# Maxima over the partitions by a TensorE product with the identity in place of a GpSimd instruction

## The chip, the core and the metric

The kernel runs on one core of a Trainium2 chip. The core has five engines that run their own queues of instructions in order and wait for each other through semaphores: TensorE (PE in the profile; its weight loads are shown apart as PEld), VectorE (DVE), ScalarE (ACT), GpSimd (POOL) and SyncE (SP, which here issues the transfers). The metric is the device time of one execution in microseconds (us).

## What is computed

Four batches of attention with eight heads, 576 tokens and head size 64, in which a score counts only if it is at most tau below its row's maximum; then a gated MLP behind an RMS norm over the 2304 tokens; then a mixture of eight experts whose weights come from a softmax over all the logits and eight Sinkhorn steps. The reference, cut to what matters:

```python
thresh = np.max(scores, axis=-1, keepdims=True) - tau
scores = np.where(scores >= thresh, scores, -1e9)
attn = softmax(scores);  x = attn @ v
xn = x / rms(x) * rms_g
x = (silu(xn @ w_gate) * (xn @ w_val)) @ w_out
P = np.exp(logits - logits.max())            # logits = x @ moe2_w_gate
for _ in range(8):                           # Sinkhorn
    P /= P.sum(1, keepdims=True) + 1e-9
    P /= P.sum(0, keepdims=True) + 1e-9
    P *= N / E
for e in range(8):
    out += P[:, e:e+1] * (np.maximum(x @ w1[e], 0) @ w2[e])
```

## The kernel before, in words

Every float32 operand of a large product is scaled by a power of two and split into two float16 parts, and three passes carry the product. The power of two comes from the largest magnitude of the operand. Along the free axis VectorE finds that maximum, one number for each of the 128 partitions (`kmm`, `vmm`, `om1`, `w1m`, `w2m`, `gm`). The maximum over the 128 partitions, with the result in all of them, is GpSimd's `partition_all_reduce` (`all_max`, L137 to L140). It is called 42 times through `all_max`: for k and v of each batch (`kmx`, `vmx`, 4 each), for w_out (`womx`), for the router's weights (`gmx`), and for w1 and w2 of each of 16 half experts (`w1mx`, `w2mx`). A 43rd call on L704 (`lgtop`) takes the maximum of the logits. From the maximum `pow2_scale` (L70 to L76) makes the scale by five small VectorE instructions; for squared norms GpSimd first takes a square root as a power (L144).

The work comes in three stages. Up to about 200 us of the span, the first batch and the MLP's weights are prepared (`prep_in`, `prep_out`). Up to about 780 us, the attention of a block of tokens is interleaved with the MLP of the block before it (`att_tile`, `mlp_block`): a score tile S on PE, its row maximum and threshold on DVE, the exponential on ACT, the float16 remainder `hl` on POOL (L271, L272), a transposing transfer to `eT`, and the product `pv` on PE; for the MLP, 12 tiles `gv` (24 matmuls each, L488) with a tanh on ACT and two DVE instructions, the remainder `tT` on POOL (L503), and two tiles `x2` (36 matmuls each, L516). From about 870 us on the mixture of experts runs: in each of 16 halves `hidden` makes tiles h (6 matmuls each, L751), and `combine` makes 18 tiles y (12 matmuls each, L797), which ACT (L808) or DVE (L812) adds up. The next half's weights are prepared meanwhile: DVE takes the row maximum (L616, L641), POOL forms sums of blocks (L621 to L624), ACT and DVE split (L604, L605).

PSUM has 8 banks. The pool `psm` gives three to the tag "mm", on which the tiles gv, x2, logits, the Sinkhorn sums cs and y take turns; the attention takes the other five (later the h tiles do). The order of instructions on each engine is made when the program is built, by a scheduler with a timeline of its own, so a change in one place moves instructions on all engines.

Of the kernel before, what the change touches and what calls it, by code (L numbers as in the profile page):

```python
# [7 lines left out]
F32 = mybir.dt.float32  # L8
# [4 lines left out]
ALU = mybir.AluOpType  # L13
# [6 lines left out]
def kernel(  # L20
# [14 lines left out]
):  # L35
    """Attention with a threshold below each row's maximum, a gated MLP behind an RMS norm, and a
    mixture of experts with Sinkhorn weights.

    Each float32 operand of a large product is scaled by a power of two, taken from its largest
    magnitude, and split into two float16 parts, hi + lo, which hold its 22 bits and more; three  # L40
    passes (hi*hi, hi*lo, lo*hi) then carry the product with float32's accuracy. The scales are
    exact, and the bounds that they give keep every float16 value finite.
    """
    nc = tc.nc
# [12 lines left out]
    NW = NCH + 1  # L57
    ABSMAX = bass_isa.ReduceOp.absmax
    MAXOP = bass_isa.ReduceOp.max

# [5 lines left out]
    def pow2_scale(mx, n, bits, name, least=2.0**-100):  # L66
        """2^(bits-1) / 2^floor(log2 mx), so that scaled values stay under 2^bits; and its inverse."""
        s = small([P, n], name + "_s")
        inv = small([P, n], name + "_i")
        V.tensor_scalar(  # L70
            inv.bitcast(I32), mx.bitcast(I32), 0x7F800000, None, ALU.bitwise_and
        )
        V.tensor_scalar(inv, inv, least, None, ALU.max)
        V.reciprocal(s, inv)
        V.tensor_scalar(s, s, 2.0 ** (bits - 1), None, ALU.mult)
        V.tensor_scalar(inv, inv, 2.0 ** (1 - bits), None, ALU.mult)  # L76
        return s, inv
# [4 lines left out]
    V.memset(half, 0.5)  # L82
    ones = small([P, P], "ones")
    V.memset(ones, 1.0)
    tau_sb = small([P, 1], "tau_sb")
    G.dma_start(out=tau_sb, in_=tau.to_broadcast([P, 1]))
# [21 lines left out]

    psm = ctx.enter_context(tc.tile_pool(name="psm", bufs=3, space=PSUM))

# [6 lines left out]

# [1 line left out]
    def load_batch(b, which="kqv"):  # L119
# [16 lines left out]

    def all_max(col, n, name):  # L137
        m = small([P, n], name, bufs=2)
        G.partition_all_reduce(m, col, P, ABSMAX)
        return m  # L140

    def norm_scale(sq, n, bits, name):
        """The scale and its inverse from squared norms."""
        G.tensor_tensor(sq, sq, half.to_broadcast([P, n]), ALU.pow)  # L144
        return pow2_scale(sq, n, bits, name, 2.0**-60)

    def row_norms(r, name):
        """Of each row of r, the largest of the squared norms of its parts."""
        r = r.rearrange("p h c d -> p (h c d)")
# [13 lines left out]
    def prep_kq(b, raws):  # L163
        kr, qr = raws
        st = {}
        s_k, i_k = norm_scale(all_max(row_norms(kr, "km"), 1, "kmx"), 1, 10, f"k{b}")
        qm = small([P, NW], "qm", bufs=2)
# [5 lines left out]
        s_q, i_q = norm_scale(qm, NW, 9, f"q{b}")  # L173
        # of a row's maximum M: -c2 M, the bias of its exponentials, and M - c1, its threshold
        wt = small([P, NW, 2], f"wt_{b}")
# [28 lines left out]
    def prep_v(b, st, vr):  # L204
        s_v, i_v = norm_scale(all_max(row_norms(vr, "vm"), 1, "vmx"), 1, 14, f"v{b}")
        vs = pa.tile([P, 2, H, NW, D], F16, tag="vs", name=f"vs{b}")
        A.activation(vs[:, 0], vr, AF.Copy, scale=s_v[:, 0:1])
        V.scalar_tensor_tensor(
            vs[:, 1].rearrange("p h c d -> p (h c d)"),
            vr.rearrange("p h c d -> p (h c d)"),  # L210
            s_v[:, 0:1],
            vs[:, 0].rearrange("p h c d -> p (h c d)"),
            ALU.mult,
            ALU.subtract,
        )
        st["vs"] = vs
        st["i_v"] = i_v
# [22 lines left out]
    def att_tile(b, c, st, qT, qX, heads, pv, sums, slot):  # L240
        """One 128-row tile of scores: 128 tokens of one head, or the last 64 of two heads."""
        kT, vs = st["kT"], st["vs"]
# [24 lines left out]
        )  # L267
        # columns: hi of keys 0..575 | lo of keys 512..575 | lo of keys 0..511
        hl = pa.tile([P, 2 * S], F16, tag="hl", name=f"hl{b}_{c}_{heads[0]}", bufs=3)
# [26 lines left out]
    def finish_x(i, x, ivx):  # L296
        """RMS norm of the 128 tokens of tile i, split and transposed."""
        ssq = pa.tile([P, 1], F32, tag="ssq", name=f"ssq{i}", bufs=2)
# [15 lines left out]

    # tiles of 128 tokens in the order in which they are made: 128 of a batch (token p * 4 + c), or
    # the last 64 of two batches
    tiles = []
# [47 lines left out]

# [1 line left out]
    wg = pw.tile([P, 2, KD, DFF], F16, tag="wg", name="wg")  # L367
# [6 lines left out]
    def words(src, name):  # L374
        """128 x DM float64 numbers, as pairs of words: the lower, the upper."""
        r = pw.tile([P, 4, 2, 2 * P], F16, tag="tT", name=name, bufs=4)
# [4 lines left out]
    def to_f32(dst, word, name):  # L381
        """Their float32, from their bits.

        2^-112 times the upper word, read as float32, has the exponent rebiased for float32 and
        three places too low; the lower word gives the last three bits of the mantissa.
        """
        lw = pw.tile([P, 2, 2, HD], F16, tag="xs", name=name, bufs=2)
# [11 lines left out]
    def prep_in(src, w, gi, name):  # L399
        """DM columns of w_gate or w_val, times rms_g, scaled for columns of norm under 2^9."""  # L400
        bits = src.bitcast(I32)
# [38 lines left out]
    def prep_out():  # L440
        """w_out, its rows scaled against their columns of w_gate and w_val."""
        bits = moe_w_out.bitcast(I32)
# [15 lines left out]
        V.tensor_reduce(om1, om, AX.X, ALU.max)  # L458
        s, inv = pow2_scale(all_max(om1, 1, "womx"), 1, 8, "wout")
        V.tensor_scalar(ixs, inv, 2.0**10, None, ALU.mult)  # L460
# [16 lines left out]
    def passes(n):  # L477
        """(part of the stationary operand, part of the moving one, chunk) of a split product."""
        return [(l, r, c) for c in range(n) for l, r in ((0, 0), (0, 1), (1, 0))]

    def mlp_block(j, pool=None):
# [30 lines left out]
        for a in range(2):  # L512
# [22 lines left out]
            xs.append(x)  # L535
        # the operands of the products below, from [B11; B21], the first tile, and [B12; B22]
        xl, xr = xs
# [27 lines left out]

# [1 line left out]
    for i, (b, c) in enumerate(tiles):  # L567
# [23 lines left out]

# [1 line left out]
    # Its first layer by Winograd's form of Strassen's product: w1[e]' = A and x' = B are cut in  # L593
    # 2 x 2, and 7 products of their blocks' sums give the 4 blocks of A B. Half an expert's F at
    # a time. Columns of B: a pair of tiles; the sums of B are those that mlp_block kept.
    pb_cm = tc.tile_pool(name="pb", bufs=1, side="left", reuse_waits="tile")
# [5 lines left out]
    def split(dst, src, s):  # L602
        """dst[:, ..., 0, :], dst[:, ..., 1, :] = the float16 parts of src * s."""
        A.activation(dst[0], src, AF.Copy, scale=s)  # L604
        V.scalar_tensor_tensor(dst[1], src, s, dst[0], ALU.mult, ALU.subtract)  # L605

    def prep_w1(h, pool):
# [8 lines left out]
        V.tensor_reduce(m, r, AX.XY, ALU.max, apply_absolute_value=True)  # L616
        s, inv = pow2_scale(all_max(m, 1, "w1mx"), 1, 3, f"w1_{h % 3}")
        a11, a12 = r[:, 0:2, 0:HF], r[:, 2:4, 0:HF]
# [14 lines left out]
    def prep_w2(h):  # L633
# [7 lines left out]
        V.tensor_reduce(m, r, AX.XY, ALU.max, apply_absolute_value=True)  # L641
        s, inv = pow2_scale(all_max(m, 1, "w2mx"), 1, 8, f"w2_{h % 3}")
        split((w[:, 0], w[:, 1]), r, s[:, 0:1])
# [26 lines left out]
    def sinkhorn():  # L670
        """Softmax over all the logits, then rows and columns brought to equal sums in turn."""
        gr = small([P, KD, E], "gr")
        nc.scalar.dma_start(out=gr, in_=moe2_w_gate.rearrange("(k p) e -> p k e", p=P))
        gm = small([P, 1], "gm")
        V.tensor_reduce(gm, gr, AX.XY, ALU.max, apply_absolute_value=True)
        s, inv = pow2_scale(all_max(gm, 1, "gmx"), 1, 8, "gate2")
        wg2 = small([P, KD, 2, E], "wg2", F16)
        A.activation(wg2[:, :, 0], gr, AF.Copy, scale=s[:, 0:1])
        V.scalar_tensor_tensor(wg2[:, :, 1], gr, s[:, 0:1], wg2[:, :, 0], ALU.mult, ALU.subtract)
        ps = psm.tile([P, NTL, 2, E], F32, tag="mm", name="logits")  # L680
        # (operand, chunk of D) whose sum is the tile's x
        parts = (
# [19 lines left out]
        V.tensor_reduce(mx, lg, AX.XY, ALU.max)  # L702
        top = small([P, 1], "lgtop")
        G.partition_all_reduce(top, mx, P, MAXOP)  # L704
        V.tensor_scalar(top, top, -1.0, None, ALU.mult)
# [37 lines left out]
    def hidden(h, g):  # L743
        """The split relu(w1[e]' x') of KH chunks of F: those of the first tiles, of the second."""
        w, xb = weights[h][0], xop[g]
# [126 lines left out]
```

## Time and profile before

| | us |
|---|---|
| median of 3 runs | 2316.86 |
| lowest and highest | 2316.15, 2324.15 |
| span of the profiled execution, first to last instruction | 2318.3 |
| PE busy | 2041.2 (88%) |
| DVE busy | 1532.4 (66%) |
| ACT busy | 817.5 (35%) |
| POOL busy | 583.1 (25%) |

The page gives the profiled execution by its span alone; it lies 1.4 us above the median of the runs, so differences in the span can be taken as differences in time. A busy share is an average over stages: POOL's 25% is gathered in the first third and in bursts later. "issue" as the releaser of a wait means that the engine sat idle and no semaphore that the profile shows explains it.

### The profile page before, as it was taken

To read this page: it belongs to the slowest core of one execution; us is meant where nothing else is said; L and a number is where in the kernel's file an instruction comes from. 1 tells how busy PE (TensorE), PEld (TensorE's weight loads), DVE (VectorE), ACT (ScalarE), POOL (GpSimd) and SP (SyncE) were. 2 spreads that over 40 slices of the span, in tenths; PEclk is the share of its full clock that TensorE was granted. 3 is DMA by queue.
4 is the path that set the end of the run, shared out by engine and by line. 5 is a ranking of instruction groups with operands and counts; after the bars stand their busy time and mean duration, and the time that the engine had idled before them with its cause. 6 is when DMAs were issued, how large, how long until landed. Compare 5 with 4: busy or idle time off the path is not lost.

```text
span 2318.3 us, 35265 instructions
## 1 busy us (share of the span) xinstructions
PE 2041.2 (88%) x13828; PEld 1195.3 (52%) x13828; DVE 1532.4 (66%) x3102; ACT 817.5 (35%) x1450; POOL 583.1 (25%) x677
## 2 busy tenths in 40 slices
PE   1234887888899797799999999999999999999999
PEld 0023675576677564354555555555555555555554
DVE  6797676677777326586676676676676676676555
ACT  4556665575565223222122122122122122122111
POOL 4675465456565322101010010010010010010000
PEclk9998999999999899799999999999999999999999
DMA  7684775785575604100010010010010010010001
GB/s 213 164 197 89 130 157 99 136 151 110 101 132 108 129 17 119 55 17 21 19 37 19 19 37 19 19 37 19 19 37 19 19 37 19 19 37 1 1 27 56
DMA packets 321879, 154.10 MB, mean 66 GB/s; under 512 B 278960, under 2 KB 292400, under 8 KB 321712
## 3 DMA queue, kind: packets, MB, share of 16 engines
q1 hardware_dynamic: 321120, 151.82, 28.9%
q8 instruction: 108, 1.77, 0.3%
q14 instruction: 59, 0.48, 0.1%
q10 hardware_dynamic: 528, 0.02, 0.0%
q0 software_dynamic: 64, 0.00, 0.0%
HBM read 68.18 MB, written 12.98 MB: 35 GB/s over the span
## 4 chain that ended last, share of the span: by engine, by line
PE 63%; issue 3%; DVE 2%; POOL 1%; DMA 1%; ACT 0%; SPq 0%; POOLq 0%; ACTq 0%; DVEq 0%
PE y L797 31%; PE h L751 26%; PE gv L488 3%; PE x L516 2%; DMA w1r<-in_moe_w_dram 1%; DMA eT<-hl 0%; POOL w1s L621 0%; DVE nt L259 0%; PE S L248 0%; DVE mx L257 0%; SPq L653 0%; DVE w L605 0%; PE pv L286 0%; DVE e L265 0%; POOL w1s L623 0%
## 5 line engine op out<-in xcount | busy, mean ns | idle before, releaser
L751 PE MATMUL h<-x2T,w 128*128 128x384 f16 x4032 | 687.9, 326 | 16.4 <-ACT u L765 15.2
L751 PEld LDWEIGHTS <-w 128*128 128x128 f16 x4032 | 394.6, 98 | 298.5 <-issue 18.0
L812 DVE SCALAR_TENSOR_TENSOR acc<-y,coef,acc 128x512 f32<-128x512 f32 x270 | 193.6, 747 | 252.0 <-PE y L797 249.9
L797 PE MATMUL y<-w,hA 128*128 128x512 f16 x864 | 221.8, 382 | 2.1 <-ACT w L604 1.6
L797 PE MATMUL y<-w,hC 128*128 128x512 f16 x864 | 211.2, 381 | 9.7 <-ACT acc L808 9.7
L797 PE MATMUL y<-w,hD 128*128 128x512 f16 x864 | 217.3, 381 | 0.0
L739 ACT ACTIVATE hA<-u 128x384 f16<-128x384 f32 x96 | 50.2, 523 | 456.9 <-DVE u L767 449.4
L797 PE MATMUL y<-w,hB 128*128 128x512 f16 x864 | 210.3, 379 | 0.0
L621 POOL TENSOR_TENSOR w1s<-w1r 128x512 f32<-128x512 f32 x16 | 23.7, 1482 | 737.8 <-DMA w1r<-in_moe_w_dram 722.2
L271 POOL TENSOR_TENSOR hl<-e,hl 128x512 f16<-128x512 f32 x144 | 174.0, 1209 | 121.7 <-ACT hl L270 60.3
L488 PE MATMUL gv<-xnT,wg 128*128 128x256 f16 x1296 | 171.4, 277 | 13.7 <-ACT x2f L534 13.7
L516 PE MATMUL x<-wo,tT 128*128 128x512 f16 x648 | 155.3, 397 | 18.7 <-POOL tT L503 18.7
L488 PE MATMUL gv<-xnT,wv 128*128 128x256 f16 x1296 | 169.6, 274 | 0.0
L248 PE MATMUL S<-kT,qT 128*128 128x288 f16 (+1 forms) x320 | 67.9, 315 | 103.2 <-DVE e L265 73.5
L488 PEld LDWEIGHTS <-wg 128*128 128x128 f16 x1296 | 127.0, 99 | 33.0 <-issue 14.6
L264 ACT ACTIVATE e<-S,nt,c 128x576 f32<-128x576 f32 x144 | 117.3, 824 | 71.5 <-DVE nt L259 60.5
L797 PEld LDWEIGHTS <-hC 128*128 128x128 f16 x864 | 84.7, 98 | 106.9 <-issue 11.1
L797 PEld LDWEIGHTS <-hB 128*128 128x128 f16 x864 | 84.7, 98 | 102.5 <-issue 0.8
L797 PEld LDWEIGHTS <-hD 128*128 128x128 f16 x864 | 84.9, 98 | 98.5 <-issue 2.2
L488 PEld LDWEIGHTS <-wv 128*128 128x128 f16 x1296 | 125.5, 98 | 16.1 <-issue 0.7
L797 PEld LDWEIGHTS <-hA 128*128 128x128 f16 x864 | 85.0, 99 | 94.3 <-issue 4.8
L265 DVE SCALAR_TENSOR_TENSOR e<-S,nt,e 128x576 f32<-128x576 f32 x144 | 115.9, 811 | 26.8 <-ACT e L264 25.9
(237 smaller groups left out, 2884.7 us busy)
## 6 DMA issues: line engine op xcount, KB each, us to landing
w1r<-in_moe_w_dram SPq DMA_DIRECT2D x16, 1024.0 KB, 5.1
w2r<-in_moe_w_dram SPq DMA_DIRECT2D x16, 1024.0 KB, 5.4
wgatew<-in_moe_w_gate_dram SPq DMA_DIRECT2D x12, 512.0 KB, 4.9
wvalw<-in_moe_w_val_dram SPq DMA_DIRECT2D x12, 512.0 KB, 4.2
wo<-in_moe_w_out_dram SPq DMA_DIRECT2D x12, 512.0 KB, 4.4
x2d<-xs SPq DMA_DIRECT2D x24, 256.0 KB, 2.5
qX<-qT SPq DMA_DIRECT2D x40, 128.0 KB, 2.5
raw_k<-in_k_dram SPq DMA_DIRECT2D x4, 1024.0 KB, 7.6
```

The lines of the kernel that those rows point to most:

```text
L248: T.matmul(sp[i * rows : (i + 1) * rows, j, 0:HS], lhsT=qq[:, h, 0:rows], rhs=kT[2 * h // H][:, h % (H // 2), j * HS : (j + 1) * HS], star ...
L264: A.activation(ev, sv, AF.Exp, bias=nt[:, 0:1], scale=st["c2"][:, c : c + 1])
L265: V.scalar_tensor_tensor(ev, sv, nt[:, 1:2], ev, ALU.is_ge, ALU.mult, accum_out=sums[:, slot : slot + 1])
L271: G.tensor_tensor(hl[:, S + REM :], e[:, 0 : NCH * P], hl[:, 0 : NCH * P], ALU.subtract)
L488: T.matmul(gv[:, a, :], lhsT=w[:, l, kk, f * P : (f + 1) * P], rhs=xt[:, r * KD + kk, :], start=n == 0, stop=n == 3 * KD - 1,)
L516: T.matmul(ps, lhsT=tT[f][:, l, o : o + P], rhs=wo[:, f, r, :], start=n == 0, stop=n == 3 * KF - 1,)
L621: G.tensor_tensor(sm[:, 0], a21, a22, ALU.add)
L739: A.activation(t[:, 0, :], src, AF.Relu)
L751: T.matmul(ps, lhsT=w[:, a, l, kk, f * P : (f + 1) * P], rhs=xb[:, b * 4 + r * 2 + kk, :], start=n == 0, stop=n == 5,)
L797: T.matmul(ps, lhsT=hs[a][f][:, l, jj * P : (jj + 1) * P], rhs=w2[:, r, f, :], start=n == 0, stop=n == 3 * KH - 1,)
L812: V.scalar_tensor_tensor(acc[i], ps, coef[h][:, i : i + 1], acc[i], ALU.mult, ALU.add)
```

## The change

`all_max` and the maximum of the logits go over to a new helper, `over_partitions`. It multiplies the column, broadcast along the free axis, with the identity on TensorE; each partition of the PSUM result then holds all 128 values in a row, and a VectorE reduction takes their maximum. For the scales the column is read as bfloat16 (the upper half of each float32: the exponent is the same), for the logits as float32. The identity is made by GpSimd at the start (`ident`, a memset and an `affine_select`), another, in float32, before the logits (`eye`). The products get a PSUM bank of their own (tag "mx"), and the tag "mm" goes from three banks to two. `ones` becomes a broadcast column.

```diff
-    ones = small([P, P], "ones")
+    ones = small([P, 1], "ones")
     V.memset(ones, 1.0)
+    ones = ones.to_broadcast([P, P])
+
+    def identity(dst):
+        G.memset(dst, 0.0)
+        G.affine_select(
+            out=dst, in_=dst, compare_op=ALU.not_equal, fill=1.0, base=0,
+            pattern=[[-1, P]], channel_multiplier=1,
+        )
+        return dst
+
+    ident = identity(small([P, P], "ident", BF16))
...
-    psm = ctx.enter_context(tc.tile_pool(name="psm", bufs=3, space=PSUM))
+    psm = ctx.enter_context(tc.tile_pool(name="psm", bufs=2, space=PSUM))
+
+    def over_partitions(col, eye, name):
+        ps = psm.tile([P, P], F32, tag="mx", name=name + "p", bufs=1)
+        T.matmul(ps, lhsT=col.to_broadcast([P, P]), rhs=eye, start=True, stop=True)
+        m = small([P, 1], name, bufs=2)
+        V.tensor_reduce(m, ps, AX.X, ALU.max)
+        return m
+
+    def all_max(col, name):
+        return over_partitions(col.bitcast(BF16)[:, 1:2], ident, name)
...
-    def all_max(col, n, name):
-        m = small([P, n], name, bufs=2)
-        G.partition_all_reduce(m, col, P, ABSMAX)
-        return m
...
-        top = small([P, 1], "lgtop")
-        G.partition_all_reduce(top, mx, P, MAXOP)
+        eye = identity(pc.tile([P, P], F32, tag="eye", name="eye"))
+        top = over_partitions(mx, eye, "lgtop")
```

The calls of `all_max` lose their second argument. In the changed kernel the lines behind the helper stand some 16 lines lower (L751 becomes L767, L797 becomes L813, L622 becomes L638).

Three places show how the instructions move. The first is POOL's queue in the passage from the MLP to the experts, where the first halves' weights are prepared; each row is a line of the kernel, an operation and its tiles. An `ISA` row with tiles is the reduction itself, one without tiles stands before it and behind it. Before:

```order
L139 ISA
L139 ISA w1mx<-w1m 128x1
L622 ISA
L622 TENSOR_TENSOR w1r_11219<-w1r_11219 128x2x256
L139 ISA
L139 ISA w2mx<-w2m 128x1
L621 ISA
L621 TENSOR_TENSOR w1s_12310<-w1r_12296 128x512
L623 TENSOR_TENSOR w1s_12310<-w1s_12310,w1r_12296 128x512
L139 ISA
L139 ISA w1mx<-w1m 128x1
L622 ISA
```

After the change, the same place in POOL's queue:

```order
L637 TENSOR_TENSOR w1s_11262<-w1r_11246 128x512
L639 TENSOR_TENSOR w1s_11262<-w1s_11262,w1r_11246 128x512
L640 TENSOR_TENSOR w1s_11262<-w1r_11246,w1s_11262 128x512
L638 TENSOR_TENSOR w1r_11246<-w1r_11246 128x2x256
L637 TENSOR_TENSOR w1s_12352<-w1r_12336 128x512
L639 TENSOR_TENSOR w1s_12352<-w1s_12352,w1r_12336 128x512
L638 TENSOR_TENSOR w1r_12336<-w1r_12336 128x2x256
L640 TENSOR_TENSOR w1s_12352<-w1r_12336,w1s_12352 128x512
```

All `ISA` rows are gone there; in POOL's whole queue of the changed kernel one is left besides those at the program's start and end, in front of the first `affine_select`.

The second place is PE's queue in the steady part of the experts, where half 6 is computed and half 8's weights are prepared. Before, three y tiles of half 6 stand within an h tile (of each tile's matmuls one row is shown, the others and the weight loads are left out):

```order
L751 MATMUL h_1_0_63_16094<-x2T_10472,w_6_15262 128x384
...
L797 MATMUL y_1_15956<-w_6_15291,hC_0_0_15827 128x512
...
L797 MATMUL y_3_15970<-w_6_15291,hC_0_0_15827 128x512
...
L797 MATMUL y_5_15984<-w_6_15291,hC_0_0_15827 128x512
...
L751 MATMUL h_1_0_26_16105<-x2T_10472,w_6_15262 128x384
```

After the change a weight load and a matmul for the maximum stand in the queue, between an h tile and a y tile:

```order
L767 LDWEIGHTS w_6_15318
L767 MATMUL h_1_0_26_16169<-x2T_10497,w_6_15318 128x384
L123 LDWEIGHTS w1m
L123 MATMUL w1mxp<-ident,w1m 128x128
L813 LDWEIGHTS hA_0_0_15856
L813 MATMUL y_4_16002<-w_6_15349,hA_0_0_15856 128x512
```

PE's queue gains 43 such pairs. It also interleaves y and h otherwise: before, 149 stretches of PE's queue hold three y tiles in a row without an h tile between them; after, none but one holds more than two, and 134 hold one.

The third place is DVE's queue at the same point. Before, the first instruction of `pow2_scale` reads what POOL has written:

```order
L812 SCALAR_TENSOR_TENSOR acc_12007<-y_16_14971,coef,acc_12007 128x512
L70 TENSOR_SCALAR w_1_i<-w1mx 128x1
L769 TENSOR_TENSOR u_5_0_0_15032<-h_0_0_35_15061,u_5_0_0_15031 128x384
L740 SCALAR_TENSOR_TENSOR hA_0_0_15058<-u_5_0_0_15030,hA_0_0_15058 128x384
L73 TENSOR_SCALAR w_1_i<-w_1_i 128x1
```

After the change a reduction from PSUM stands in front of it:

```order
L125 TENSOR_REDUCE w1mx<-w1mxp 128x1
L792 TENSOR_TENSOR u_6_1_0_16109<-h_1_0_26_16169,u_6_1_0_16109 128x384
L790 TENSOR_TENSOR u_6_1_0_16108<-h_1_0_63_16158,u_6_1_0_16108 128x384
L756 SCALAR_TENSOR_TENSOR hB_1_0_16155<-u_6_1_0_16110,hB_1_0_16155 128x384
L68 TENSOR_SCALAR w_2_i<-w1mx 128x1
L828 SCALAR_TENSOR_TENSOR acc_11199<-y_4_16002,coef,acc_11199 128x512
```

DVE's queue gains 43 such reductions.

## Rows read from the trace of the kernel before

**Rows 1.** The page: busy tenths of PE in 40 equal slices of the span.

```profile
PE   1234887888899797799999999999999999999999
```

**Rows 2.** Line L139 (`partition_all_reduce`): durations (minimum, median, maximum), waits until, waiters.

```profile
L139 POOLq MODIFY_POOL_CONFIG  x80: 1/10/37, 3.0 to 2065.7; - x80
...
  issue: 136.1, 22
...
  DVE w_i L70: 100.8, 28
```

**Rows 3.** Timeline of POOL around 190 us: start, duration, instruction, [idle before <-releaser].

```profile
189.09 0.41 POOL L139 PARTITION_ALL_REDUCE womx<-om  x1 [6.13 <-issue]
189.42 0.43 POOL L139 PARTITION_ALL_REDUCE kmx<-kmm  x1
196.85 0.59 POOL L144 TENSOR_TENSOR kmx<-kmx,half 128x1 f32<-128x1 f32 x1 [6.99 <-issue]
```

**Rows 4.** Timeline of PE: the instructions behind its nine longest waits after 70 us.

```profile
83.91 0.66 PE L248 MATMUL S<-kT,qT 128*128 128x288 f16 x2 [18.28 <-DVE e L265]
...
199.80 0.66 PE L248 MATMUL S<-kT,qT 128*128 128x288 f16 x2 [12.13 <-DVE k_i L73]
...
284.46 9.45 PE L516 MATMUL x<-wo,tT 128*128 128x512 f16 x34 [5.60 <-POOL tT L503]
...
366.06 0.66 PE L248 MATMUL S<-kT,qT 128*128 128x288 f16 x2 [11.22 <-DVE e L265]
...
451.30 9.01 PE L516 MATMUL x<-wo,tT 128*128 128x512 f16 x31 [5.44 <-POOL tT L503]
...
531.88 1.89 PE L516 MATMUL x<-wo,tT 128*128 128x512 f16 x4 [7.68 <-POOL tT L503]
...
778.86 2.72 PE L488 MATMUL gv<-xnT,wg 128*128 128x256 f16 x12 [13.73 <-ACT x2f L534]
...
927.06 2.72 PE L797 MATMUL y<-w,hC 128*128 128x512 f16 x6 [9.73 <-ACT acc L808]
...
967.27 1.12 PE L751 MATMUL h<-x2T,w 128*128 128x384 f16 x3 [15.21 <-ACT u L765]
```

**Rows 5.** Waits: who <- for whom: us in total, times, longest.

```profile
DVE v_i L70 <- POOL vmx L144: 41.9, 4, 14.5
DVE k_i L70 <- POOL kmx L144: 39.1, 4, 12.6
```

**Rows 6.** The chain that ended last, 745 to 1030 us: start, duration, what.

```profile
761.25 7.38 issue
...
769.11 7.11 issue
```

**Rows 7.** Four windows: length, busy us of PE, PEld, DVE, ACT, POOL; clock, DMA share, GB/s.

```profile
100.00:150.00 50.00, 18.32 (x138) 10.14 (x139) 50.00 (x95) 23.77 (x38) 39.04 (x36) 1.00 0.90 211
900.00:950.00 50.00, 37.54 (x325) 19.72 (x325) 24.58 (x43) 14.10 (x22) 12.21 (x9) 0.83 0.21 64
950.00:1000.00 50.00, 34.16 (x190) 18.97 (x189) 33.35 (x81) 12.30 (x22) 7.48 (x8) 0.86 0.06 21
1100.00:1150.00 50.00, 50.00 (x263) 25.57 (x262) 29.54 (x55) 7.56 (x15) 1.64 (x2) 1.00 0.07 22
```

**Rows 8.** Timeline 829 to 831 us: what reads a gv tile; PE's next tile.

```profile
829.46 1.47 PE L488 MATMUL gv<-xnT,wg 128*128 128x256 f16 x12
...
829.72 0.47 ACT L496 ACTIVATE u<-gv,g 128x256 f32<-128x256 f32 x1 [0.26 <-PE gv L488]
...
830.68 0.42 DVE L498 SCALAR_TENSOR_TENSOR u<-u,gv 128x256 f32<-128x256 f32 x1
...
832.08 1.47 PE L488 MATMUL gv<-xnT,wg 128*128 128x256 f16 x12
```

**Rows 9.** Timeline of DVE, two instructions of the expert stage.

```profile
1044.27 2.29 DVE L641 TENSOR_REDUCE w2m<-w2r 128x1 f32<-128x2048 f32 x1
...
1047.40 0.74 DVE L812 SCALAR_TENSOR_TENSOR acc<-y,coef,acc 128x512 f32<-128x512 f32 x1
```

More of the change, by code (lines that the diff above doesn't have):

```diff
@@ L4 @@
 import concourse.tile as tile
-from concourse import bass_isa, mybir
+from concourse import mybir
 from concourse._compat import with_exitstack
@@ L57 @@
     NW = NCH + 1
-    ABSMAX = bass_isa.ReduceOp.absmax
-    MAXOP = bass_isa.ReduceOp.max
     p0 = ctx.enter_context(tc.tile_pool(name="p0", bufs=1, side="left"))
@@ L165, in prep_kq @@
         st = {}
-        s_k, i_k = norm_scale(all_max(row_norms(kr, "km"), 1, "kmx"), 1, 10, f"k{b}")
+        s_k, i_k = norm_scale(all_max(row_norms(kr, "km"), "kmx"), 1, 10, f"k{b}")
         qm = small([P, NW], "qm", bufs=2)
@@ L204, in prep_v @@
     def prep_v(b, st, vr):
-        s_v, i_v = norm_scale(all_max(row_norms(vr, "vm"), 1, "vmx"), 1, 14, f"v{b}")
+        s_v, i_v = norm_scale(all_max(row_norms(vr, "vm"), "vmx"), 1, 14, f"v{b}")
         vs = pa.tile([P, 2, H, NW, D], F16, tag="vs", name=f"vs{b}")
@@ L458, in prep_out @@
         V.tensor_reduce(om1, om, AX.X, ALU.max)
-        s, inv = pow2_scale(all_max(om1, 1, "womx"), 1, 8, "wout")
+        s, inv = pow2_scale(all_max(om1, "womx"), 1, 8, "wout")
         V.tensor_scalar(ixs, inv, 2.0**10, None, ALU.mult)
@@ L616, in prep_w1 @@
         V.tensor_reduce(m, r, AX.XY, ALU.max, apply_absolute_value=True)
-        s, inv = pow2_scale(all_max(m, 1, "w1mx"), 1, 3, f"w1_{h % 3}")
+        s, inv = pow2_scale(all_max(m, "w1mx"), 1, 3, f"w1_{h % 3}")
         a11, a12 = r[:, 0:2, 0:HF], r[:, 2:4, 0:HF]
@@ L641, in prep_w2 @@
         V.tensor_reduce(m, r, AX.XY, ALU.max, apply_absolute_value=True)
-        s, inv = pow2_scale(all_max(m, 1, "w2mx"), 1, 8, f"w2_{h % 3}")
+        s, inv = pow2_scale(all_max(m, "w2mx"), 1, 8, f"w2_{h % 3}")
         split((w[:, 0], w[:, 1]), r, s[:, 0:1])
@@ L675, in sinkhorn @@
         V.tensor_reduce(gm, gr, AX.XY, ALU.max, apply_absolute_value=True)
-        s, inv = pow2_scale(all_max(gm, 1, "gmx"), 1, 8, "gate2")
+        s, inv = pow2_scale(all_max(gm, "gmx"), 1, 8, "gate2")
         wg2 = small([P, KD, 2, E], "wg2", F16)
```

## The prediction

> **What bounds the kernel now.** I read the page's slices first: from the slice at about 1000 us on PE is busy in all tenths; the room is in the first 1000 us [rows 1]. The windows say it in numbers: 50.00 of 50 us from 1100 to 1150, at a granted clock of 1.00, but 37.54 and 34.16 between 900 and 1000, at 0.83 and 0.86, so partly at the lower of its two levels [rows 7].
>
> Then the changed line. The reduction itself runs some 0.4 us [rows 3], but around it the trace has 80 MODIFY_POOL_CONFIG, and 22 of the reductions waited 136.1 us for nothing but "issue" [rows 2]. The timeline of POOL shows what that is: 6.13 us of nothing before two reductions, 6.99 us of nothing behind them, before POOL's next ordinary instruction [rows 3]. 43 reductions, three of which share a pair of configurations with a neighbour, make 40 such pairs, so POOL is out for 13 us 40 times, some 520 us. Ordinary POOL work, and whoever needs it, is held as well.
>
> Third, PE's waits: the nine longest after 70 us [rows 4] all fall where POOL is out. In some the releaser is POOL's tT, in others a DVE instruction, behind which DVE itself had waited for kmx or vmx, eight times, 81.0 us together [rows 5]; the wait of 13.73 us is an ACT instruction queued behind work that needs POOL, and the chain shows POOL's two outages of 7.38 and 7.11 us in it [rows 6]. In the steady stage POOL's outages cost nothing, since PE is never idle there.
>
> **The change part by part.** The price of one new maximum: a matmul of 128 columns and a DVE reduction of 128 by 128. The steady window has 263 matmuls of 384 or 512 columns in 50.00 us, 0.19 us each [rows 7]; a shorter one costs between nothing and that. The nearest DVE instruction on PSUM takes 0.74 us for 512 columns [rows 9]; the reduction costs between 0.1 and that. With hand-overs a maximum should take about 1 us instead of some 13.
>
> - *Preparation, to 200 us.* DVE limits this stage: 50.00 of 50 us busy from 100 to 150 [rows 7], and while it waits for kmx and vmx nothing else of its queue runs. Of its eight waits three lie here, by their means 10.5 and twice 9.8 us, 30 together [rows 5]; PE's two waits, 18.28 and 12.13, say the same, 30.4 [rows 4]. The DMA share is 0.90 in the same window, so some of it may be given back. I take 28, between 15 and 38.
> - *Attention with MLP, to 750 us.* PE's waits are 5.60, 11.22, 5.44 and 7.68, together 29.9 [rows 4]. Behind such a wait it runs slower: 34 matmuls in 9.45 us are 0.28 each, against 0.19, up to 3 us a time; I add 4 in all, up to 10. The third bank of "mm" is taken away here. A gv tile's bank is read until 831.10, 1.6 us after its product ended at about 829.46; the tile after the next starts 2.62 us later, at 832.08 [rows 8]. With two banks that leaves 1.0 us of slack where ACT and DVE are free; with attention's work queued on both, some of it overruns. I take off 8. This makes 26, between 5 and 40.
> - *The first expert's w1mx, 760 to 779.* POOL's two outages, 14.5 us, lie on the chain [rows 6], and PE waits 13.73 [rows 4]. After, POOL's sums run on. I take 12, between 8 and 14.5.
> - *Passage to the experts, 880 to 1000.* PE is idle 12.5 and 15.8 us in the two windows, 28.3 [rows 7], most of it in two waits of 9.73 and 15.21 [rows 4]; the low clock costs up to 0.17 of 37.54 and 0.14 of 34.16 more, 11 together. The order shows POOL's queue without its loads. What is late next is DVE: 57.9 us of work in these 100 [rows 7], which must then fit into some 75, with six row maxima of 2.29 us [rows 9] and the splits that wait for a transfer. I take 20, between 8 and 36.
> - *Experts, from 1000 us.* Here 28 maxima are added to a full PE, at up to 0.19 us each, 0 to 5. The wait that is new: PE's queue stands still until the row maximum is there. By the order the product stands 182 matmuls or more behind the last tile that DVE handles before that row maximum, in every half of this stage, which is 35 us at 0.19; the reduction takes 2.29. So PE finds it ready; were it late, the y and h tiles behind it would stand, and ACT and DVE with them. In turn DVE's new reduction waits for PE, and behind it stand evictions of h and y; the product has been issued some tiles before, so it is there. Only in the passage are two of them close, 37 and 38 matmuls behind, about 7 us, and there the weights' transfer decides; a few us lie inside the bounds above. DVE has 29.5 of 50 us to do and takes the 28 reductions, at most 21 us over 1300, beside PE. The y tiles lose a bank; before they ran three in a row, now at most two with h tiles between. I take a cost of 4, between 0 and 15.
> - gmx moves from the start of the program to 37 matmuls before the logits, 7 us at 0.19 each, for seven small instructions: nothing. The identity is made once at the start, while the first loads are under way; `eye` is a memset and a select in POOL's queue before the x2 sums. Both together 0 to 3 us, taken as nothing: the cover is PE's h work.
>
> 28 + 26 + 12 + 20 - 4 = 82 us off the span of 2318.3 give 2236; the median stands 1.4 below the span, so 2235.
>
> **A rule beside the rows.** POOL's outage is 6.13 us before and 6.99 behind [rows 3]. The Trainium skill's page "GPSIMD Engine Reference", section "2.1 Instruction dispatch", says that the first call to a freshly loaded kernel pays about 6 us with no visible instruction. The trace agrees on the first half; by the page alone a maximum would hold POOL 6 us instead of 13, and the sum would be about half, 41 us. The rows count both ways, and the measurement decides.
>
> **The rivals.**
> 1. *All of it comes back.* No bank is missed and DVE keeps up in the passage: 38 + 40 + 14.5 + 36 - 2 = 126, 2190. For it: each of PE's waits falls on an outage. Against it: DVE at 50.00 of 50, DMA at 0.90 [rows 7].
> 2. *Other limits stand right behind.* Preparation is held by transfers (15), the two banks eat the middle stage (0), and the passage becomes DVE's (12): 15 + 0 + 10 + 12 - 5 = 32, 2285.
> 3. *Slower: two banks bind.* There are 108 gv, 18 x2 and 288 y tiles on "mm", 414. A DVE row maximum of 2.29 us in front of an eviction of 0.74 [rows 9] holds a bank 3.0 us, longer than a tile's 2.6. If a tile waits 0.2 us on average, 83 us, the gain is gone; from there on it is slower, and at 0.35 us it is 145: 2380. Against it: the order keeps h tiles between y tiles. The Trainium skill's "Perfetto Trace Analysis", section "Identifying Performance Opportunities", says that the same gap repeating on the engine that should be saturated can mean too little PSUM. The rows before show no such gap in the steady stage, with three banks; with two no run here shows it yet.
> 4. *PE stands still for each of the 32 weight maxima* by a row maximum of 2.29 us: 73 us of the 82 are lost, 2308.
> 5. *The configurations stay*, because the select or the powers still need them: 2320. Against it: POOL's queue after shows no ISA row in front of them but one.
>
> **How the numbers follow.** The forecast, with its own range 2212 to 2258, gets 0.56, the first rival 0.14, the second 0.17, the third 0.05, the fourth 0.05, the fifth 0.03. What a measurement of this kernel can tell from no change is 0.5%, 11.6 us. Faster are the forecast and rivals 1 and 2, 0.87; the same are rivals 4 and 5, 0.08; slower is rival 3, 0.05. The range reaches from 2195 to 2285, which takes in the forecast, half of the first rival and most of the second.
>
> **What would show it.** Right: one or two MODIFY_POOL_CONFIG, POOL without waits for "issue" of 6 to 8 us, PE's nine waits gone or under 3 us, DVE's waits for kmx and vmx under 2 us, PE at 48 or more of 50 from about 960 on, and halves of the experts as long as before. Wrong in the banks: PE waits in front of gv or y for ACT's or DVE's reading of "mm", in the steady stage. Wrong in the order: PE waits at L123. Wrong in the first stage: DVE or the transfers busy in a stage that is as long as before.

## The result, and the profile after

| | before | after |
|---|---|---|
| median, us | 2318.75 (4 runs) | 2222.05 (4 runs) |
| ratio, 95% interval | | 0.9581 (0.9563 to 0.9598) |
| span of the profiled execution | 2318.3 | 2220.2 |

The change takes 97 us off, where 82 were forecast; 2222 lies in the forecast's own range of 2212 to 2258. To see where, the span is cut at five marks that both traces have: the start of the first gv matmul, of the first matmul of the eighth of nine MLP blocks, of the last x2 matmul, of the 433rd of 3456 y matmuls (the third half of the experts) and of the 3025th (the fifteenth). All numbers of the table, here and for the experiments below, are differences between such starts; preparation begins with the span, and the end runs to the start of the last y matmul.

| us | preparation | middle | tail and passage | twelve halves | end |
|---|---|---|---|---|---|
| before | 218.1 | 541.6 | 339.6 | 1050.8 | 163.2 |
| after | 185.5 | 505.4 | 311.2 | 1050.8 | 162.1 |
| gain | 32.6 | 36.2 | 28.4 | 0.0 | 1.1 |
| predicted | 28 | 26 | 12 + 20 | -4 | |

The page of the changed kernel, busy tenths of PE in 40 slices, answers to [rows 1]:

```profile
PE   1337899899999998999999999999999999999999
```

From the sixth slice on (277 us) PE is at 9, but for two slices of 8, where before there were, up to 1000 us, mostly 8 and 7. The changed lines, first the identity (L87), then the product (L123) and the reduction (L125), with durations in ns as minimum, median and maximum. Under them stands whom PE or its weight loads waited for, and who waited for them (us, times):

```profile
L87 POOLq MODIFY_POOL_CONFIG  x2: 37/37/37, 2.8 to 2.8; - x2
L123 PE MATMUL w1mxp<-ident,w1m x16: 219/219/229, 693.5 to 1977.3; 128*128 128x128 bf16 x16
...
  DVE w2m L657: 1.4, 2
  DVE w1m L632: 1.3, 2
...
  DVE w1mx L125: 4.5, 3
...
L125 DVE TENSOR_REDUCE w1mx<-w1mxp x16: 270/285/292, 693.8 to 1979.9; 128x1 f32<-128x128 f32 x16
```

One pair of configurations is left of those in [rows 2]; before there were 158 in all, 80 at L139 and 78 at the lines behind it, where POOL went back. A product is 0.22 us and a reduction 0.28. The four waits for w1m and w2m, 2.7 us, are two, each seen by the weight load and by its matmul; the matmuls alone waited 0.9 us. DVE waited three times for a product of w1mx. Of PE's waits of over 1.5 us after 200 us, four remain, against 17 before, among which are seven of [rows 4]:

```profile
300.90 0.58 PE L302 MATMUL pv<-vs,eT 128*128 128x64 f16 x14 [1.61 <-DMA eT<-hl]
...
443.86 0.58 PE L302 MATMUL pv<-vs,eT 128*128 128x64 f16 x14 [3.40 <-DMA eT<-hl]
...
703.94 6.71 PE L767 MATMUL h<-x2T,w 128*128 128x384 f16 x30 [4.49 <-DMA x2T<-x2d]
...
884.86 0.51 PE L733 MATMUL cs<-skc,ones 128*128 128x8 f32 x2 [4.46 <-DVE skc L731]
```

None of them is an outage of POOL or a wait for a maximum. The windows, with the columns of [rows 7]; the two in the middle are the passage, which lies 100 us earlier now:

```profile
100.00:150.00 50.00, 15.89 (x148) 9.80 (x145) 50.00 (x95) 32.00 (x53) 35.84 (x32) 0.53 0.74 198
800.00:850.00 50.00, 47.17 (x271) 26.09 (x270) 46.19 (x78) 22.13 (x39) 18.19 (x15) 1.00 0.55 146
850.00:900.00 50.00, 45.33 (x400) 26.35 (x399) 38.34 (x104) 15.26 (x27) 5.03 (x4) 0.97 0.13 43
1100.00:1150.00 50.00, 50.00 (x269) 26.02 (x267) 39.07 (x71) 13.24 (x23) 5.00 (x4) 1.00 0.12 42
```

In the passage PE has gone from 37.54 and 34.16 of 50 to 47.17 and 45.33, at a granted clock of 1.00 and 0.97. DVE's 46.19 is now close to its limit. Preparation still has DVE at 50.00 of 50. PE's granted clock is 0.53 there, near the lower of its two levels, where it was 1.00 before; PE has 15.89 of 50 us to do. One of the four runs had a mean clock of 0.998, which leaves the lower level some 9 us of the whole span, against some 90 in the profiled run with 0.980. It took 2222.18 against 2221.93, so the low clock there costs nothing that the times show.

The middle stage as one window each, first before, then after:

```profile
218.10:759.70 541.60, 474.84 (x5028) 353.31 (x5026) 387.11 (x925) 329.45 (x593) 303.50 (x416) 0.96 0.68 127
```

```profile
185.50:690.90 505.40, 467.86 (x5066) 351.36 (x5066) 390.22 (x935) 331.46 (x598) 308.88 (x414) 0.99 0.73 137
```

PE's idle time falls from 66.8 to 37.5 us, and its busy time by 7.0, with 38 matmuls more in the window: the granted clock was 0.96 of full speed in the mean, with 46 us at the lower of its two levels, and is 0.99 now, with 7. What is new is a small wait for the second bank, PE's waits after 200 us (sum, times, longest) in the changed kernel; no row of before has it:

```profile
PE gv L504 <- DVE u L514: 4.6, 8, 1.3
```

### The profile page after: what moved, and what is told of

Same layout as the page of the kernel before. It is cut to its first block, busy times and chain, and to the rows that moved or that the text cites. A ratio compares the mean times of both kernels' runs of the same rounds, so it can differ in the third digit from the quotient of the medians.

```text
span 2220.2 us, 35202 instructions
## 1 busy us (share of the span) xinstructions
PE 2029.6 (91%) x13872; PEld 1190.3 (54%) x13872; DVE 1547.7 (70%) x3145; ACT 818.8 (37%) x1450; POOL 546.2 (25%) x638
## 4 chain that ended last, share of the span: by engine, by line
PE 68%; DVE 12%; DMA 8%; issue 4%; ACT 3%; POOL 2%; SPq 1%; ACTq 0%; POOLq 0%; DVEq 0%
PE y L813 33%; PE h L767 28%; DMA eT<-hl 4%; PE gv L504 4%; PE x L532 2%; DVE mx L273 2%; DVE e L281 1%; DVE nt L275 1%; DMA kT<-ks 1%; DVE wo L409 1%; DMA qT<-qs 1%; ACT e L280 1%; POOL hl L287 1%; PE pv L302 1%; PE S L264 1%
## 5 line engine op out<-in xcount | busy, mean ns | idle before, releaser
L767 PE MATMUL h<-x2T,w 128*128 128x384 f16 x4032 | 703.6, 327 | 7.6 <-DMA x2T<-x2d 4.5
L767 PEld LDWEIGHTS <-w 128*128 128x128 f16 x4032 | 394.2, 98 | 297.4 <-issue 11.2
L828 DVE SCALAR_TENSOR_TENSOR acc<-y,coef,acc 128x512 f32<-128x512 f32 x270 | 198.5, 747 | 281.7 <-PE y L813 281.5
L813 PE MATMUL y<-w,hD 128*128 128x512 f16 x864 | 219.9, 379 | 0.0
L813 PE MATMUL y<-w,hA 128*128 128x512 f16 x864 | 210.6, 379 | 1.3 <-DVE acc L828 1.1
L813 PE MATMUL y<-w,hC 128*128 128x512 f16 x864 | 211.2, 381 | 0.2 <-ACT acc L824 0.2
L813 PE MATMUL y<-w,hB 128*128 128x512 f16 x864 | 210.3, 379 | 0.0
L504 PE MATMUL gv<-xnT,wg 128*128 128x256 f16 x1296 | 165.1, 275 | 11.3 <-DMA xnT<-xn 5.8
L755 ACT ACTIVATE hB<-u 128x384 f16<-128x384 f32 x96 | 50.2, 522 | 312.8 <-DVE u L787 312.0
L532 PE MATMUL x<-wo,tT 128*128 128x512 f16 x648 | 144.6, 379 | 0.3 <-DVE u L514 0.3
L813 PEld LDWEIGHTS <-hB 128*128 128x128 f16 x864 | 84.7, 98 | 102.5 <-issue 1.0
L813 PEld LDWEIGHTS <-hD 128*128 128x128 f16 x864 | 84.5, 98 | 95.3
L813 PEld LDWEIGHTS <-hC 128*128 128x128 f16 x864 | 84.9, 99 | 92.5 <-issue 1.4
L813 PEld LDWEIGHTS <-hA 128*128 128x128 f16 x864 | 84.1, 98 | 90.4 <-issue 1.8
```

Source lines behind the costliest of these rows:

```text
L504: T.matmul(gv[:, a, :], lhsT=w[:, l, kk, f * P : (f + 1) * P], rhs=xt[:, r * KD + kk, :], start=n == 0, stop=n == 3 * KD - 1,)
L532: T.matmul(ps, lhsT=tT[f][:, l, o : o + P], rhs=wo[:, f, r, :], start=n == 0, stop=n == 3 * KF - 1,)
L755: A.activation(t[:, 0, :], src, AF.Relu)
L767: T.matmul(ps, lhsT=w[:, a, l, kk, f * P : (f + 1) * P], rhs=xb[:, b * 4 + r * 2 + kk, :], start=n == 0, stop=n == 5,)
L813: T.matmul(ps, lhsT=hs[a][f][:, l, jj * P : (jj + 1) * P], rhs=w2[:, r, f, :], start=n == 0, stop=n == 3 * KH - 1,)
L828: V.scalar_tensor_tensor(acc[i], ps, coef[h][:, i : i + 1], acc[i], ALU.mult, ALU.add)
```

## The experiments

The theory was that the gain is POOL's outage leaving; the rivals, that it is VectorE's wait for the maximum, or that the stages act on each other; open were the price of the third bank and of a new maximum. In different sets of runs the kernel before had medians of 2318.75 to 2324.96, so between kernels of different sets a few us mean nothing; the ratio of each is against before in its own set.

| kernel | median | ratio (95%) | preparation | middle | tail, passage | twelve halves | end |
|---|---|---|---|---|---|---|---|
| before, two banks | 2360.27 | 1.0159 (1.0135 to 1.0183) | 217.9 | 556.9 | 348.1 | 1067.1 | 162.1 |
| shared banks | 2276.50 | 0.9792 (0.9769 to 0.9815) | 180.0 | 559.6 | 294.3 | 1067.6 | 167.6 |
| attention only | 2292.17 | 0.9864 (0.9840 to 0.9888) | 197.1 | 509.4 | 347.2 | 1070.3 | 162.1 |
| experts only | 2307.99 | 0.9932 (0.9908 to 0.9956) | 221.0 | 556.8 | 311.6 | 1050.1 | 162.1 |
| outage put back | 2352.13 | 1.0130 (1.0114 to 1.0145) | 235.0 | 568.7 | 332.5 | 1050.5 | 162.1 |
| each maximum twice | 2235.41 | 0.9624 (0.9609 to 0.9639) | 187.5 | 512.4 | 312.7 | 1051.4 | 162.2 |
| halves 3 to 15 on POOL | 2245.34 | 0.9672 (0.9656 to 0.9687) | 185.9 | 507.7 | 314.9 | 1066.4 | 162.1 |
| no maxima, two banks | 2216.51 | 0.9548 (0.9533 to 0.9564) | 184.6 | 504.8 | 310.5 | 1047.9 | 162.1 |
| no maxima, three banks | 2204.54 | 0.9492 (0.9479 to 0.9505) | 185.0 | 498.3 | 297.5 | 1050.8 | 163.2 |

**The third bank alone.**

```diff
 # the kernel before
-    psm = ctx.enter_context(tc.tile_pool(name="psm", bufs=3, space=PSUM))
+    psm = ctx.enter_context(tc.tile_pool(name="psm", bufs=2, space=PSUM))
```

> The kernel before, with two banks instead of three for the tag mm and nothing else changed: what the third bank is worth with GpSimd's maxima in place. The prediction took off 8 us for the bank in the middle stage: 2318.8 + 8 = 2327, with small gaps in front of gv and y. Rival, the bank costs nothing (in the trace after the change PE's waits in front of gv are 11.3 us in all, 5.8 of them for a transfer, and those in front of y 1.5): 2319, between 2314 and 2323. Rival of the two banks that bind (0.2 to 0.35 us a tile over 414 tiles): 2400 or more, with waits in front of y in the steady stage.

It costs 35 us, far more than the 8 and far less than the rival of 2400. By the traces, which lie 39 apart, 15 are in the middle, 8 in tail and passage, and 16 in the twelve halves, 1.36 each, where the prediction took 4 for new products and lost bank together. The waits between 1200 and 2000 us show how (who <- for whom: us in total, times, longest):

```profile
DVE w_i L70 <- POOL w1mx L139: 31.3, 8, 4.2
...
PE y L797 <- DVE acc L812: 14.2, 9, 1.9
```

DVE's wait for w1mx was there before as well (39.5 us, 9 times, in the same stretch), and cost nothing. With two banks PE runs into it, once per half. One such place in the timeline (start, duration, instruction, [idle before <-releaser]):

```profile
1376.84 0.41 POOL L139 PARTITION_ALL_REDUCE w1mx<-w1m  x1 [6.00 <-issue]
1377.29 0.15 DVE L70 TENSOR_SCALAR w_i<-w1mx 128x1 int32<-128x1 int32 x1 [3.93 <-POOL w1mx L139]
...
1380.45 1.40 DVE L812 SCALAR_TENSOR_TENSOR acc<-y,coef,acc 128x512 f32<-128x512 f32 x2
...
1381.25 1.46 PE L797 MATMUL y<-w,hC 128*128 128x512 f16 x6 [1.58 <-DVE acc L812]
```

POOL is out for 6.00 us, DVE stands 3.93 us at the scale, the evictions acc stand behind it in DVE's queue, and PE waits 1.58 us for the bank that they read. A third bank covers that wait.

**The banks shared.**

```diff
 # the changed kernel
-    psm = ctx.enter_context(tc.tile_pool(name="psm", bufs=2, space=PSUM))
+    psm = ctx.enter_context(tc.tile_pool(name="psm", bufs=3, space=PSUM))
...
-        ps = psm.tile([P, P], F32, tag="mx", name=name + "p", bufs=1)
+        ps = psm.tile([P, P], F32, tag="mm", name=name + "p")
```

> The changed kernel with three banks for the tag mm, and the products of the maxima taking turns on them instead of having one of their own. If the third bank is worth the 8 us of the prediction: 2222 - 8 = 2214. If it is worth nothing: 2222, between 2217 and 2227. Rival: a maximum's product now queues behind gv or y tiles for a bank, and holds one until VectorE has read it (0.28 us of reading); 43 times up to 2 us would be 2222 to 2300.

The rival was right, by its upper half: 54 us slower than the changed kernel by the medians and the traces, 49 by the ratios. The middle loses 54 and the halves 17, while tail and passage gain 17. The reason in the middle is the turn. The product for the second batch's keys has its column ready, but its place in PE's queue is behind gv tiles that take their turns on the same banks; PE does not wait at the product itself. In this kernel:

```profile
158.93 0.15 DVE L176 TENSOR_REDUCE kmm<-km 128x1 f32<-128x3 f32 x1
...
245.56 0.22 PE L123 MATMUL kmxp<-ident,kmm 128*128 128x128 bf16 x1
...
259.89 0.64 PE L264 MATMUL S<-kT,qT 128*128 128x288 f16 x2 [14.12 <-DMA kT<-ks]
```

And in the changed kernel:

```profile
161.25 0.15 DVE L176 TENSOR_REDUCE kmm<-km 128x1 f32<-128x3 f32 x1
...
167.44 0.22 PE L123 MATMUL kmxp<-ident,kmm 128*128 128x128 bf16 x1
```

87 us against 6 from the column to its product. The keys are scaled late, and the scores wait 14.12 us for kT, again at two later batches. PE's waits after 200 us for it, first here, then in the changed kernel:

```profile
PE S L264 <- DMA kT<-ks: 56.4, 6, 14.1
```

```profile
PE S L264 <- DMA kT<-ks: 1.6, 4, 0.6
```

The bank of its own is what lets a maximum go ahead of its turn. In each of the twelve halves PE waits once for DVE's u in front of an h tile, 1.13 us, which the changed kernel does not show; that is most of the 17, and where it comes from stays open.

**Half of the change each.** The calls in the experts and the router, or those for k, v and w_out, go to a helper that is GpSimd's instruction again; mm has two banks in both.

```diff
 # attention only
-        s, inv = pow2_scale(all_max(m, "w1mx"), 1, 3, f"w1_{h % 3}")
+        s, inv = pow2_scale(pool_max(m, "w1mx"), 1, 3, f"w1_{h % 3}")
 # the same for w2mx, gmx, lgtop
...
 # experts only
-        s_v, i_v = norm_scale(all_max(row_norms(vr, "vm"), "vmx"), 1, 14, f"v{b}")
+        s_v, i_v = norm_scale(pool_max(row_norms(vr, "vm"), "vmx"), 1, 14, f"v{b}")
 # the same for kmx, womx
```

> The changed kernel, but the maxima of the experts (w1, w2, the router's weights, the logits) go back to GpSimd; those of k, v and w_out stay on TensorE. By the terms of the prediction only the two first are kept, 28 and 26: 2318.8 - 54 = 2265. By the milestones of the two traces (the first gv tile 32.6 us earlier, the middle stage 36.2 shorter) 2318.8 - 69 = 2250. Rival, the passage to the experts would have been shorter also without its own maxima on TensorE, since it meets other work: under 2240. Rival, the stages make up for each other: above 2275.

> The changed kernel, but the maxima of k, v and w_out go back to GpSimd; those of the experts and the router stay on TensorE. By the terms of the prediction w1mx and the passage are kept, 12 and 20, and 4 are lost: 2318.8 - 28 = 2291. By the milestones of the two traces (8.4 in the tail of the MLP, 20.0 in the passage, 1 afterwards) 2318.8 - 29 = 2289. If the gains add up, what this kernel and its counterpart lose against the changed one comes to 97 us together; under 80 or over 115 would mean that the stages act on each other.

By the numbers both expectations end at stages that act on each other: together the two lose 156 us against the changed kernel, not 97. That is not the reason. I had compared them with the kernel before; but they have two banks, so they belong beside the kernel before with two. From there attention only gains 68 us, experts only 52, and the whole change 138. By stages the parts add up: in the middle 47.5 and 0.1 against 51.5, in tail and passage 0.9 and 36.5 against 36.9, in the twelve halves -3.2 and 17.0 against 16.3. Only preparation does not: 20.8 and -3.1 against 32.4. POOL's start in "attention only" tells why:

```profile
13.74 0.28 POOL L87 TENSOR_SCALAR_AFFINE_SELECT ident<-ident 128x128 bf16<-128x128 bf16 x1 [10.79 <-issue]
19.98 0.41 POOL L130 PARTITION_ALL_REDUCE gmx<-gm  x1 [5.96 <-issue]
27.47 0.59 POOL L164 TENSOR_TENSOR kmx<-kmx,half 128x1 f32<-128x1 f32 x1 [7.08 <-issue]
```

The router's maximum is taken at the start here, and its outage, in and out, stands ahead of the first keys' power at 27.47; in the changed kernel that power starts at 14.82, and the first scores 12 us earlier (41.7 against 53.5). So gmx is not free at the start once kmx is gone from POOL.

**POOL's outage, with nobody waiting for its result.**

```diff
 # the changed kernel
+    def outage(col):
+        m = small([P, 1], "unread", bufs=2)
+        G.partition_all_reduce(m, col, P, bass_isa.ReduceOp.absmax)
...
-        s_k, i_k = norm_scale(all_max(row_norms(kr, "km"), "kmx"), 1, 10, f"k{b}")
+        kx = all_max(row_norms(kr, "km"), "kmx")
+        s_k, i_k = norm_scale(kx, 1, 10, f"k{b}")
+        outage(kx)
 # the same for v, w_out, w1 and w2, not for the router and the logits
```

> The changed kernel, with GpSimd's reduction run 41 times more, behind each maximum (of k and v behind the power that makes the scale), on the same number or column, into a tile that nothing reads. It puts POOL's outages back, but nothing waits for their result: VectorE has its maxima at once. With both parts back and two banks the kernel before took 2360. If what the change removes is VectorE's wait for the maximum (outage and reduction in the way of the scale): 2222 to 2245, and halves of the experts of 87.6 us. If it is POOL's absence itself (the remainders hl and tT and the sums w1s come late, whoever needs the maximum): 2320 or more in the stages before the experts. My estimate from the waits of PE, of which some end on POOL's tT or ACT behind POOL and some on VectorE: 2265 to 2300, all of the loss before 1000 us, and none in the halves.

2352, near the 2360 of the kernel before with two banks: in sum the outage alone takes back all of the gain before the experts. By stages it does not put back what was there. Measured from the changed kernel, the outage costs 49.5 us in preparation and 63.3 in the middle, where the kernel before with two banks is 32.4 and 51.5 longer; in tail and passage it costs 21.3 where that kernel is 36.9 longer. Whether the other 16 are VectorE's wait for the maximum or the order of the queues is not told apart. My estimate of 2265 to 2300 was too low, since I counted only the waits that end on POOL's own tiles. POOL around 210 us:

```profile
199.16 0.41 POOL L130 PARTITION_ALL_REDUCE unread<-om  x1 [5.96 <-issue]
206.91 0.59 POOL L163 TENSOR_TENSOR kmx<-kmx,half 128x1 f32<-128x1 f32 x1 [7.34 <-issue]
...
214.77 0.41 POOL L130 PARTITION_ALL_REDUCE unread<-kmx  x1 [5.87 <-issue]
222.63 1.14 POOL L294 TENSOR_TENSOR hl<-e,hl 128x512 f16<-128x512 f32 x1 [7.45 <-issue]
```

and PE in the same stretch:

```profile
211.82 0.93 PE L309 MATMUL pv<-vs,eT 128*128 128x64 f16 x14 [14.41 <-DMA eT<-hl]
...
226.94 0.93 PE L309 MATMUL pv<-vs,eT 128*128 128x64 f16 x14 [13.24 <-DMA eT<-hl]
```

The releaser that PE names is a transfer; what is late is hl on POOL, which the transfer carries. VectorE has its maxima at once, but it still waits 66 us for other results of POOL: 12 each for the powers of kmx and qm, which stand behind an outage, and most for a power in the attention, for which it waited 1.9 us in the kernel before:

```profile
DVE rs L328 <- POOL rs L327: 41.4, 7, 13.9
```

So the run shows what POOL's absence can cost with nobody waiting for the maximum; it does not divide the loss of the kernel before between its waiters. The twelve halves are as short as in the changed kernel, 1050.5: there the outage itself costs nothing, and only a DVE that waits for its result does.

**The halves on POOL again.**

```diff
 # the changed kernel
-        s, inv = pow2_scale(all_max(m, "w1mx"), 1, 3, f"w1_{h % 3}")
+        s, inv = pow2_scale((pool_max if h > 2 else all_max)(m, "w1mx"), 1, 3, f"w1_{h % 3}")
 # the same for w2mx
```

> The changed kernel, but the maxima of w1 and w2 of halves 3 to 15 go back to GpSimd; all others stay on TensorE, and mm keeps two banks. The prediction held that GpSimd's maxima cost nothing in the steady stage, since PE is never idle there, and priced the new ones at 4 us: 2218 to 2222. The theory after the first four runs: VectorE waits some 4 us for w1mx in each half, with evictions of y behind it; three banks hide that, two do not, so that each half takes 1.4 to 1.6 us more, as in the two kernels that had two banks and GpSimd's maxima there: 13 times 1.5 is 20, 2238 to 2246, with one wait of PE in front of y for VectorE's acc in each half. Rival, those halves were longer because the passage had another order: 2222.

2245, and 1.30 us more per half: the theory. Its waits between 1200 and 2000 us:

```profile
DVE w_i L68 <- POOL w1mx L130: 34.5, 9, 4.0
...
PE y L817 <- DVE acc L832: 12.8, 9, 1.6
```

The last row, in the changed kernel, is one wait of 0.5. So of the two parts of the change, one would have lost 16 us in these halves, and the other takes away what loses them.

**The price of a maximum, from above and below.** Taken twice (the second product reads the first one's result), or not at all:

```diff
 # each maximum twice
-        return over_partitions(col.bitcast(BF16)[:, 1:2], ident, name)
+        for i in range(2):
+            col = over_partitions(col.bitcast(BF16)[:, 1:2], ident, name + "a" * (1 - i))
+        return col
...
 # no maxima
-        ps = psm.tile([P, P], F32, tag="mx", name=name + "p", bufs=1)
-        T.matmul(ps, lhsT=col.to_broadcast([P, P]), rhs=eye, start=True, stop=True)
         m = small([P, 1], name, bufs=2)
-        V.tensor_reduce(m, ps, AX.X, ALU.max)
+        V.tensor_copy(m, col)
...
```

> The changed kernel, each maximum through all_max taken twice in a row: the second product takes the result of the first reduction, so the number is the same, and each costs another weight load, matmul and reduction and their hand-overs. In the profile after the change the matmul takes 0.22 us and the reduction 0.28, with hand-overs about 1 us. If the price of a maximum lies beside other work, as its 16 pairs in the steady stage suggest: 2222 to 2227. If each counts with its matmul on a full PE: 28 of 0.1 to 0.22, 2225 to 2228. Rival, the hand-overs lie on the path in preparation and attention, where VectorE limits: 9 to 14 times 1 to 2 us, 2232 to 2250. Rival, PE's queue stands still at the second product for VectorE each time: 42 times 1 to 2 us, 2264 or more.

> The changed kernel without its maxima over partitions: a copy of one number on VectorE stands in place of the product and its reduction, so each partition gets its own scale and the output is not the reference's. mm keeps two banks. The difference to the changed kernel is all that the new maxima cost. If they lie beside other work: 2217 to 2222. If they cost as much as a second one did in the kernel with each maximum taken twice (13 us for 41): 2205 to 2213. The prediction's about 1 us each, all on the path, would be 43 us less: 2180.

Twice costs 13 us more by the medians and 10 by the ratios, by the table 7 of them in the middle. That lies in the first rival's range of 2232 to 2250, not in the 2222 to 2228 that I expected: a second product and its hand-overs are partly on the path there. Taking them away gives 5.5 us, at the edge of what can be told apart (the intervals of the two ratios touch). A half has two products; it goes from 87.33 us without them to 87.56 with them and 87.62 with four, so 0.12 us for each of the first, 0.03 for each further one. In the experts the maxima are all but free.

**The third bank without outages.**

```diff
 # no maxima, as above
...
-    psm = ctx.enter_context(tc.tile_pool(name="psm", bufs=2, space=PSUM))
+    psm = ctx.enter_context(tc.tile_pool(name="psm", bufs=3, space=PSUM))
```

> The same kernel without maxima over partitions, its output as little the reference's, and with three banks for mm, which it can have because no product needs one. The difference to its counterpart with two is what the third bank is worth where GpSimd has no outages. The prediction took 8 us. With GpSimd's maxima the bank was worth 36 us. Theory: what the third bank hides is waits for POOL's outages, so without them it is worth little: 0 to 5 us less than the counterpart. Rival, it is worth the same 36 us here, so that the change gave up 36 us: 30 us or more less than the counterpart.

12 us by the medians and 15 by the traces, between the 0 to 5 of the theory and the rival's 36: a miss of the theory. In the middle it is 6.5. PE's waits after 200 us name it, with two banks

```profile
PE gv L502 <- ACT x2f L548: 6.9, 2, 4.7
PE gv L502 <- DVE u L512: 4.2, 6, 1.3
```

and with three

```profile
PE gv L502 <- ACT x2f L548: 2.2, 2, 1.9
...
PE gv L502 <- DVE u L512: 1.0, 1, 1.0
```

7.9 us less at gv. The rest lies in tail and passage (13.0 less), and 4.0 come back in the halves and the end. In tail and passage it need not all be a wait, since with three banks y and h tiles stand in another order; how much of it is which stays open. The middle stage of this kernel, to be set beside the two windows above:

```profile
185.00:683.30 498.30, 465.23 (x5040) 351.19 (x5038) 385.79 (x931) 326.55 (x592) 304.26 (x411) 0.99 0.75 138
```

As a whole the gain of 97 us is then some 114 to 118 from the maxima off POOL (2204.54 against before), some 5 to 8 back for the new ones, and 12 back for the bank.

## Why the prediction was right, by its steps

- *What bounds the kernel: POOL's outages.* Right, and shown for the sum: with the outages alone put back, the gain is gone. Of PE's waits the reading was too broad. Two of 6.86 and 6.14 us, in front of scores at 168.54 and 135.72, are longer than two of the nine in [rows 4], and POOL is not out there; both end on VectorE's e, and waits of that kind and size are in preparation after the change too (7.38 and 7.07 us). The Trainium skill's page "GPSIMD Engine Reference", section "2.1 Instruction dispatch", speaks of about 6 us at the first call to a freshly loaded kernel. The rows shown of the outage put back agree, with 5.96 and 5.87, and have 7.34 and 7.45 on the way back as well, which the section does not speak of; the sum that is half as large for that reason, 41, is ruled out by the 97.
- *Preparation, 28.* 32.6. The term counted DVE's three waits only; part of the rest is gmx, which the prediction moved "for nothing". Only together with kmx does its leaving count: the first scores start at 41.7 instead of 47.6.
- *Middle, 34 less 8.* 36.2; this is the term that was mis-sized most. The bank was right, 6.5 for 8, by the kernels without maxima. The gain was too small: without maxima and with three banks the stage is 43.3 us shorter, not 34. PE's idle time falls there by 33.7 (29.9 were taken, the long waits alone), and its busy time by 9.6, where I had 4 for the low clock: I priced the clock by one stretch behind one wait, and the whole stage had 46 us at the lower level.
- *First w1mx and passage, 12 and 20.* 28.4, by two errors against each other, so that its closeness is luck. Maxima off POOL are worth 42.1 here with three banks; the second bank, which the sum charged to the middle alone, takes 13.0 back.
- *Experts, -4.* 0.0 for the twelve halves and 1.1 at the end. The 24 products there cost 2.9, inside the estimate; a plan with two banks orders h and y otherwise and is 2.9 shorter (1047.9 against 1050.8, both without maxima). That the two cancel is luck. The sentence that POOL's outages cost nothing in the steady stage was true only for three banks: with two, the maxima on POOL cost 1.3 to 1.6 us a half. I weighed the bank and the outage apart, and they hang together.
- *The rivals.* Two banks that bind: the mechanism exists, an eviction held up in DVE's queue and PE behind it, but what holds it up is mostly the wait for POOL, and that leaves with the same change. 12 us over 414 tiles are 0.03 each, not the 0.2 of its break-even. The Trainium skill's "Perfetto Trace Analysis", section "Identifying Performance Opportunities", says that a gap which repeats on the engine that should be saturated can mean too little SBUF or PSUM. The kernel before with two banks has just that gap, 1.3 to 1.9 us once per half, and the rows agree that a bank closes it; but the changed kernel closes it with two banks, by taking away what DVE waits for. PE standing still for the weight maxima: 0.9 us, not 73. Configurations that stay: 2 of 158. All of it coming back: without maxima and with three banks it would have been 114 to 118 of 126.
- *What would show it.* PE at 48 of 50 came from 900 us on rather than 960, and the halves are 87.56 against 87.57. Three of PE's waits after 200 us are above the 3 us that I allowed for the old ones, for eT, x2T and the Sinkhorn sums, 12 us together. VectorE's waits for kmx and vmx came down from 81.0 us to 0.7. A wait of POOL for "issue" of 8.35 us in front of a remainder xs is in both kernels, so that sign was too broad.

## What to carry to other kernels

An instruction that takes its engine out is to be priced by all that is queued behind it on that engine, not by who waits for its result: here the outage cost some 130 us with nobody waiting for it (2352 against 2222). A buffer that hides a wait and the wait itself belong in one term; give up the buffer only together with what it hides (even then it was worth 12 us here), and compare a half of such a change with the kernel that has the same buffers. Short urgent work needs a buffer of its own: here sharing three banks was some 50 us slower than having two and one.

## What the runs showed of the hardware

- GpSimd's reduction takes 0.41 us, but in the kernel before mostly 5.8 to 6.2 us pass before it and 6.7 to 8.2 behind it. Where nothing reads its result the rows have 5.9 to 7.6 and 6.7 to 9.5.
- The affine_select at 2.90 us starts with no gap in the changed kernel. In three kernels with GpSimd reductions it starts 10.6 to 10.8 us after the instruction before it ("attention only", the outage put back, the halves on POOL), but in "experts only", which has them too, 0.34 us after. What decides is not shown.
- A product of 128 by 128 in bfloat16 shows 0.22 us, and in a full PE queue it costs 0.12 us or less. With float32 columns (the logits) it is two weight loads of 0.19 and two matmuls of 0.27 us.
